# A packed block's second half one fill later, and the kept rows stored one a turn

## The chip, the cores and the metric

The kernel runs on one core of a Trainium2 chip. The metric is the device time of one execution in microseconds. The core has a matrix engine (PE), a vector engine (DVE), an activation engine (ACT), a GpSimd engine and a synchronising engine (SP). In this kernel SP issues all loads and ACT all stores; sixteen DMA engines move the data of both.

## The reference

`x` is one picture of 384 x 384 positions with 384 channels, in bf16 (113 MB). Every channel is averaged and maximised over all positions, a small two-layer network turns the two vectors into one scale per channel, and the picture is multiplied by it.

```python
def reference(x, w1, w2):
    B, H, W, C = x.shape
    xf = x.reshape(B, H * W, C)
    gap = jnp.mean(xf, 1)
    gmp = jnp.amax(xf, 1)
    h_a = gap @ w1
    h_a = h_a * (h_a > 0)
    ...
    scale = _sigmoid(h_a @ w2 + h_m @ w2)
    return x * scale[:, None, None, :]
```

## The kernel before

The 147,456 positions are laid over 128 partitions, 1152 "rows" in each. One row is 768 bytes in each partition, 98,304 bytes in all. The scale is known only when all rows have been seen, and not all rows fit on the chip, so there are two passes: pass one loads everything and keeps as much as it can; pass two multiplies and stores what was kept, and loads the rest again.

**Pass one.** The tile `body` has 96 rows of ring (three slots of 31 rows and a few spare) and seven homes of 24 rows. A list `steps` is written in order by hand; SP issues its loads, PE adds up each loaded piece (`sums`, L258), DVE takes its maximum into `acc` (L324). A slot is loaded again when PE's sums and DVE's maxima over its last contents are done. Loads into the ring are called fills.

Besides the ring there are seven packed blocks (`PACKED`) of 32 rows: 24 go into `homes[i]`, eight into `fourth[i]`, a part of the tile `held`. ACT tests each block (`test`, L285 and L286, three calls) whether its bytes may be packed. PE and ACT then pack it in two halves: `pack(i, half)` is 24 matmuls into the PSUM tile `words_ps` (L306), two ACT copies (L312) and one ACT instruction that reads `words_ps` out (L313). There is one `words_ps`, so PE can begin the second half only behind L313 of the first. After packing, 32 rows lie in 24. All engines run in program order, so where `pack(i, 1)` stands in `steps` sets what PE does before it. Between the blocks stand the fills of `BETWEEN`: the last block (i = 6) is followed by fills of 30 and 27 rows; then come those of `PASSING` (25 rows; 22; 21 and 10 in one slot; 8 and 17 in one slot). From there on slots are loaded for good, piece by piece (`STAYING`, `LAST_HELD`).

Some rows are also kept in PSUM: `kept_ps` (8 rows), `kept_b` (2 rows) and `late` (8 rows, transposed).

**Between the passes** the maximum is folded, the network is evaluated and `scale_bc` is made (L416).

**Pass two.** First the rows that stayed are multiplied and stored. Then 25 turns follow. Turn t multiplies the next reloaded block (L421), stores it (L473), issues every further load whose place is free (`read`, L508), and does that turn's jobs: unpacking a half of a packed block (`unpack`, L451 to L470), or `finish`, which multiplies an unpacked block (24 rows in its home, eight in `held`) and stores it. The sizes and places in `body` of the reloaded blocks are in `PLACES`; the last turns have 48 (turn 18), 48, 48, 48, 36, 30 and 20 rows (turn 24). Block 5 is finished in turn 18, block 6 unpacked in turns 17 and 19 and finished in turn 21. The rows from PSUM are brought back in turn 22: multiplied into rows 222 to 240 of `body`, which lie in the home of block 5. Their three stores and the two of block 6 are issued in the last turn (24), ahead of that turn's own store.

Every DMA signals on one of eight semaphores. The program gives them out in turn, so that a DMA also waits until the one that last had its semaphore has landed.

Of the kernel before, what the change touches and what calls it, by code (L numbers as in the profile page):

```python
# [17 lines left out]
U32 = mybir.dt.uint32  # L18
# [16 lines left out]
PACKED = 7  # L35
PSUM_ROWS = 8
# [22 lines left out]
)  # L59
LEAVING_AT = 222  # L60
FIRST_STORES = ((1, 2, 3, 4, 4, 5, 6, 6), (9, 10, 12), (16, 18))
HELD_STORES = (6, 7)
ACC_STORES_AT = 3
# [6 lines left out]
def kernel(  # L70
# [7 lines left out]
    nc = tc.nc  # L78
# [14 lines left out]
    def rows_of(ap, block):  # L93
        first, n = block
        return ap[first * P:(first + n) * P, :].rearrange("(p n) c -> p n c", n=n)
# [8 lines left out]
    def take(n):  # L104
        nonlocal at
        at += n
        return at - n, n

    ps_block = take(PSUM_ROWS)
    beside = take(BANK_ROWS + A)  # L110
    packed_block = take(GP * PACKED)
    held_block = take(sum(LAST_HELD))
# [7 lines left out]
    again = [take(n) for _, n in PLACES]  # L120
# [25 lines left out]
    body = xpool.tile([P, RING + 3 * G * PACKED, C], BF16, name="body")  # L146
# [13 lines left out]
    kept_ps = psum.tile([P, PSUM_ROWS, C], BF16)  # L160
    words_ps = psum.tile([P, G, C], BF16)
    words = words_ps.rearrange("p n c -> p (n c)").bitcast(F32)
    late = words_ps[:, 0:LATE_ROWS, :]
# [7 lines left out]
    kept_b = bank_b[:, 0:C * BANK_ROWS // 2].bitcast(BF16).rearrange("p (n c) -> p n c", n=BANK_ROWS)  # L171
# [31 lines left out]
    def fill(*parts):  # L203
        nonlocal n_slot
        j = 0
        for block, lo, hi in parts:
            steps.append(("load", block, slots[n_slot % NS][:, j:j + hi - lo, :], lo, hi))
            j += hi - lo
            assert j <= SLOT
        n_slot += 1  # L210

    def whole(block):
        return block, 0, block[1]

    for i in range(PACKED):
        first, d_at = 3 * G * i, 3 * G * PACKED + G * i
        for lo, hi in ((0, FIRST_LOAD), (FIRST_LOAD, 3 * G)) if i == 0 else ((0, 3 * G),):
            steps.append(("load", packed_block, homes[i][:, lo:hi, :], first + lo, first + hi))
        steps.append(("load", packed_block, fourth[i], d_at, d_at + G))
        steps += [("test", i, 0), ("pack", i, 0), ("test", i, 1), ("test", i, 2)]  # L220
        for k, b in enumerate(between[i]):
            if i == 0 and k == 0:
                fill(whole(ps_block), whole(beside), whole(b))
            else:
                fill(whole(b))
            if k == 0:
                steps.append(("pack", i, 1))
    for k, b in enumerate(passing[:-1]):
        if k == SHARED_FILL:
# [96 lines left out]
    def turn_over(out_, rows):  # L326

        for r in range(LATE_ROWS):
            for q in range(CQ):
                nc.tensor.transpose(  # L330
                    out=out_[:, r, q * P:(q + 1) * P], in_=rows[:, r, q * P:(q + 1) * P], identity=ident_bf
                )
# [11 lines left out]
    for st in steps:  # L344
# [8 lines left out]
        _, block, rows, lo, hi = st  # L353
# [9 lines left out]
        j = max(0, min(m, A - done))  # L363
# [41 lines left out]
    for q0, part_ps in tp_ps:  # L405
        n = part_ps.shape[1]
# [12 lines left out]
    def multiply(dst, src):  # L419
        n = dst.shape[1]  # L420
        nc.vector.tensor_tensor(  # L421
            out=dst, in0=src, in1=scale_bc.unsqueeze(1).to_broadcast([P, n, C]), op=ALU.mult
        )

    def put(block, buf, pieces, lo=0):
        j = 0
        for m in pieces:
            rows = buf[:, j:j + m, :]
            multiply(rows, rows)
            nc.scalar.dma_start(out=rows_of(orr, block)[:, lo + j:lo + j + m, :], in_=rows)  # L430
            j += m

    def put_acc():
        for lo, hi in acc_pieces:
            multiply(acc[:, lo:hi, :], acc[:, lo:hi, :])
            nc.scalar.dma_start(out=acc_rows(orr, lo, hi), in_=acc[:, lo:hi, :])


    turns = len(PLACES)
# [32 lines left out]
    def store(buf, block, lo):  # L472
        nc.scalar.dma_start(out=rows_of(orr, block)[:, lo:lo + buf.shape[1], :], in_=buf)  # L473
# [3 lines left out]
    def finish(i):  # L477

        for rows in (homes[i], homes_d[i]):
            multiply(rows, rows)  # L480
        if i < PACKED - 1:
            store_block(i)

    def store_block(i):
        store(homes[i], packed_block, 3 * G * i)
        store(homes_d[i], packed_block, d_at + G * i)


    jobs = [[(unpack, 0, 0)], [(unpack, 0, 1)]]
    for i in range(1, PACKED):  # L490
        jobs += [[(unpack, i, 0)], [(finish, i - 1)], [(unpack, i, 1)]]
    jobs += [[], [(finish, PACKED - 1)]]

    order = []
    turn_of_row = [-1] * (RING + 3 * G * PACKED)

    def read(last_turn, blocks_gone):

        if not again:
            return False  # L500
        k = len(PLACES) - len(again)
        lo, n = PLACES[k]
        if lo + n > RING + 3 * G * blocks_gone or max(turn_of_row[lo:lo + n]) > last_turn:
            return False
        turn_of_row[lo:lo + n] = [k] * n
        buf, b = body[:, lo:lo + n, :], again.pop(0)
        assert b[1] == n
        nc.sync.dma_start(out=buf, in_=rows_of(xr, b))  # L508
        order.append((b, buf))
        return True  # L510

    k = ACC_STORES_AT
    put(stay[0], slots[0], FIRST_STORES[0][:k])
    put_acc()
    j = sum(FIRST_STORES[0][:k])
    put(stay[0], slots[0][:, j:, :], FIRST_STORES[0][k:], j)
    put(held_block, held[:, LATE_ROWS:, :], HELD_STORES, LATE_ROWS)
    put(refill, held[:, 0:LATE_ROWS, :], (LATE_ROWS,))
    read(-1, 0)
    put(stay[1], slots[1], FIRST_STORES[1])  # L520
    read(-1, 0)
    put(stay[2], slots[2], FIRST_STORES[2])
    read(-1, 0)
# [4 lines left out]
    leaving = []  # L528
    gone = 0
    for turn in range(turns):  # L530
        b, buf = order.pop(0)
        multiply(buf, buf)
        if turn == turns - 1:
            for to, block, rows in leaving:
                store(to, block, 0)
            store_block(PACKED - 1)
        store(buf, b, 0)
        while read(turn, gone):
            pass
        for job, *which in jobs.pop(0) if jobs else ():  # L540
            job(*which)
            gone += job is finish
        if turn == turns - 3:
            j = LEAVING_AT
            assert j >= max(lo + n for lo, n in PLACES) and gone > PACKED - 2
            for block, rows in ((held_block, late), (ps_block, kept_ps[:, 0:PSUM_ROWS, :]), (beside, kept_b)):
                n = rows.shape[1]
                to = body[:, j:j + n, :]
                if block == held_block:
                    nc.vector.tensor_copy(out=to.bitcast(U32), in_=rows.bitcast(U32))  # L550
                    turn_over(rows, to)
                leaving.append((to, block, rows))
                j += n
            assert j <= RING + 3 * G * (PACKED - 1)
            for to, block, rows in leaving[1:] + leaving[:1]:
                multiply(to, rows)
    assert not again and not order
    with tc.If(bad != 0):
        for i in range(PACKED):
            for buf, lo in ((homes[i], 3 * G * i), (homes_d[i], d_at + G * i)):  # L560
                n = buf.shape[1]
# [33 lines left out]
```

## Time and profile before

| | us |
|---|---|
| median of 3 runs (734.73 to 735.58) | 735.13 |
| the profiled execution, its own time | 735.08 |
| its span, first to last instruction | 733.3 |
| DVE busy | 563.3 |
| ACT busy | 348.7 |
| PE busy (matmuls) | 187.4 |

The profile's lines are read so: each instruction carries the line of the program that made it, the tile it writes and reads, and its shape; "[2.99 <-DMA ...]" is the time for which its engine stood idle before it, and what ended that. A load or store is seen at its issue, and its landing is told from the issue on. The span begins with the first instruction; 1.8 us of the profiled execution's time lie around it.

### The profile page before, as it was taken

The numbers are of one execution on the slowest core, as the hardware profiler recorded it, in microseconds if no ns is written. First come the engines' busy times: TensorE is split into PE (matmuls) and PEld (weight loads), VectorE is DVE, ScalarE is ACT, GpSimd is POOL, SyncE is SP. The second block draws the span as 40 slices with busy tenths as digits, with TensorE's granted clock in tenths as the row PEclk, the third lists the DMA queues.
The fourth block names the chain that finished last, engine by engine and source line by source line (L and its number), as shares of the span: only waits on it lengthen the run. The fifth ranks groups of instructions, "written<-read, shape, count | busy, mean of one in ns | idle before, by whom it ended". The sixth has DMA issues, their size and how long they took to land.

```text
span 733.3 us, 3860 instructions
## 1 busy us (share of the span) xinstructions
PE 187.4 (26%) x1357; PEld 74.5 (10%) x1357; DVE 563.3 (77%) x421; ACT 348.7 (48%) x251; POOL 0.7 (0%) x6
## 2 busy tenths in 40 slices
PE   5655578676667561000000000000000000001000
PEld 2222223232222130000000000000000000001000
DVE  6799999999998998959999594985866790599110
ACT  6979999999999000046245335081080062000000
POOL 0000000000000000000000000000000000000000
PEclk9989878798977555555555555555555555555555
DMA  9999999999998988999999999999999999999996
GB/s 379 435 422 425 433 430 428 431 428 427 424 430 336 424 345 333 387 431 434 433 430 434 424 438 433 427 436 426 435 431 439 423 444 427 421 434 433 424 422 276
DMA packets 21987, 305.63 MB, mean 417 GB/s; under 512 B 2800, under 2 KB 3408, under 8 KB 9552
## 3 DMA queue, kind: packets, MB, share of 16 engines
q1 hardware_dynamic: 13328, 192.14, 62.0%
q10 hardware_dynamic: 8640, 113.25, 36.3%
q8 instruction: 10, 0.16, 0.1%
q14 instruction: 9, 0.07, 0.0%
HBM read 192.14 MB, written 113.25 MB: 416 GB/s over the span
## 4 chain that ended last, share of the span: by engine, by line
DMA 54%; DVE 18%; another core or an unknown queue 9%; ACT 7%; PE 5%; issue 2%; SPq 0%; ACTq 0%; DVEq 0%
DMA body<-in_x_dram 32%; DMA out_dram<-body 22%; DVE acc L324 8%; DVE body L421 8%; PE words_ps L306 4%; ACT body L312 2%; ACT held L285 2%; ACT held L286 1%; PE bank_a L258 1%; ACT body L313 1%; DVE held L421 0%; ACT body L470 0%; ACT held L470 0%; DVE acc L421 0%
## 5 line engine op out<-in xcount | busy, mean ns | idle before, releaser
L421 DVE TENSOR_TENSOR body<-body,scale_bc 128x9216 bf16<-128x9216 bf16 (+15 forms) x45 | 214.7, 4803 | 106.4 <-DMA body<-in_x_dram 103.6
L324 DVE TENSOR_TENSOR acc<-acc,body 128x2304 bf16<-128x2304 bf16 (+4 forms) x210 | 229.8, 1166 | 17.3 <-DMA body<-in_x_dram 17.3
L470 ACT COPY held<-body 128x1536 uint8<-128x1536 uint8 x14 | 20.6, 1475 | 201.4 <-DMA out_dram<-held 130.6
L258 PE MATMUL bank_a<-body,small 128*1 128x512 bf16 (+2 forms) x849 | 85.6, 453 | 67.4 <-DMA body<-in_x_dram 67.4
L330 PE MATMUL words_ps<-ident_bf,body 128*128 128x128 bf16 x24 | 2.7, 309 | 387.6 <-DVE body L550 387.6
L286 ACT ACTIVATE held<-held 128x3072 uint8<-128x3072 uint8 (+1 forms) x35 | 82.0, 2343 | 1.1
L285 ACT ACTIVATE held<-body,held 128x3072 uint8<-128x3072 int8 (+1 forms) x28 | 61.9, 2211 | 10.3 <-DMA body<-in_x_dram 9.8
L306 PE MATMUL words_ps<-body,scale_bc 128*128 128x512 fp8e4 (+1 forms) x126 | 40.4, 436 | 24.4 <-ACT body L313 24.4
L258 PEld LDWEIGHTS <-small 128*1 128x1 bf16 x891 | 29.5, 93 | 125.9 <-issue 107.0
L330 PEld LDWEIGHTS <-body 128*128 128x128 bf16 x24 | 2.5, 143 | 387.9 <-issue 387.9
L470 ACT COPY body<-acc 128x1536 uint8<-128x1536 uint8 x28 | 41.2, 1472 | 0.4
L306 PE MATMUL words_ps<-body,w_sb 128*128 128x512 fp8e3 x84 | 28.1, 419 | 0.0
L306 PE MATMUL words_ps<-held,body 128*128 128x512 fp8e4 x84 | 27.3, 409 | 0.0
L470 ACT COPY held<-acc 128x1536 uint8<-128x1536 uint8 x14 | 20.6, 1472 | 7.2 <-DVE acc L456 7.2
L470 ACT COPY body<-body 128x1536 uint8<-128x1536 uint8 x14 | 20.7, 1475 | 0.4
L312 ACT COPY body<-held 128x1536 uint8<-128x1536 uint8 x14 | 20.6, 1469 | 0.0
L470 ACT COPY acc<-body 128x1536 uint8<-128x1536 uint8 x14 | 20.5, 1466 | 0.0
L312 ACT COPY body<-body 128x1536 uint8<-128x1536 uint8 x14 | 20.4, 1460 | 0.0
L313 ACT ACTIVATE body<-words_ps 128x1536 uint16<-128x1536 f32 x14 | 20.1, 1439 | 0.0
L285 ACT ACTIVATE held<-held 128x3072 uint8<-128x3072 int8 x7 | 20.0, 2855 | 0.2
L306 PEld LDWEIGHTS <-scale_bc 128*128 128x128 bf16 x126 | 13.1, 107 | 46.9 <-issue 36.9
L324 DVE TENSOR_TENSOR acc<-acc,held 128x1920 bf16<-128x1920 bf16 (+4 forms) x18 | 17.5, 1008 | 0.1
(70 smaller groups left out, 183.2 us busy)
## 6 DMA issues: line engine op xcount, KB each, us to landing
body<-in_x_dram SPq DMA_DIRECT2D x20, 2976.0 KB, 21.7
out_dram<-body ACTq DMA_DIRECT2D x17, 2304.0 KB, 29.6
body<-in_x_dram SPq DMA_DIRECT2D x16, 2304.0 KB, 17.9
body<-in_x_dram SPq DMA_DIRECT2D x4, 4608.0 KB, 27.8
out_dram<-body ACTq DMA_DIRECT2D x4, 4608.0 KB, 47.3
body<-in_x_dram SPq DMA_DIRECT2D x6, 2880.0 KB, 20.1
body<-in_x_dram SPq DMA_DIRECT2D x5, 3456.0 KB, 20.2
out_dram<-body ACTq DMA_DIRECT2D x5, 3456.0 KB, 43.1
```

The source lines that it names most:

```text
L258: nc.tensor.matmul(sum_ps[q * QP:q * QP + 1, 0:g * P], lhsT=ones_bf[:, 0:1], rhs=rows[:, k:k + g, q * P:(q + 1) * P], start=(done + k == 0 ...
L285: nc.scalar.activation(out=out_, in_=rows, func=ACT.Square, bias=test_bias, scale=TEST_SCALE)
L286: nc.scalar.activation(out=out_, in_=out_, func=ACT.Square, bias=minus4, accum_out=tests[:, k:k + 1],)
L306: nc.tensor.matmul(words[:, c:c + BANK], lhsT=weights[2 * r + k], rhs=high(part(i, r), dt)[:, half * n + c:half * n + c + BANK], start=(r ...
L312: nc.scalar.copy(out=high(part(i, r), U8)[:, span], in_=low(part(i, r + 2), U8)[:, span])
L313: nc.scalar.activation(out=part(i, 2).rearrange("p n c -> p (n c)").bitcast(U16)[:, span], in_=words, func=ACT.Copy, bias=32767.5,)
L324: nc.vector.tensor_tensor(out=out_, in0=in0, in1=in1, op=ALU.max)
L330: nc.tensor.transpose(out=out_[:, r, q * P:(q + 1) * P], in_=rows[:, r, q * P:(q + 1) * P], identity=ident_bf)
L421: nc.vector.tensor_tensor(out=dst, in0=src, in1=scale_bc.unsqueeze(1).to_broadcast([P, n, C]), op=ALU.mult)
L470: nc.scalar.copy(out=dst, in_=src)
```

## The change

In pass one the second half of a block's packing is put behind the second fill after the block, where it stood behind the first. In pass two the rows from PSUM are multiplied three turns earlier (turn 19), in another order of places; their stores are issued one a turn in turns 20, 21 and 22, each behind that turn's own store; and block 6 is stored where it is finished, in turn 21. The last turn stores its own block alone.

```diff
+LEAVING_TURN = 19
...
-            if k == 0:
+            if k == 1:
                 steps.append(("pack", i, 1))
...
         for rows in (homes[i], homes_d[i]):
             multiply(rows, rows)
-        if i < PACKED - 1:
-            store_block(i)
-
-    def store_block(i):
         store(homes[i], packed_block, 3 * G * i)
         store(homes_d[i], packed_block, d_at + G * i)
...
         multiply(buf, buf)
-        if turn == turns - 1:
-            for to, block, rows in leaving:
-                store(to, block, 0)
-            store_block(PACKED - 1)
         store(buf, b, 0)
+        if leaving:
+            to, block = leaving.pop(0)
+            store(to, block, 0)
         while read(turn, gone):
             pass
...
-        if turn == turns - 3:
+        if turn == LEAVING_TURN:
             j = LEAVING_AT
-            for block, rows in ((held_block, late), (ps_block, kept_ps[:, 0:PSUM_ROWS, :]), (beside, kept_b)):
+            for block, rows in ((ps_block, kept_ps[:, 0:PSUM_ROWS, :]), (held_block, late), (beside, kept_b)):
                 n = rows.shape[1]
-                to = body[:, j:j + n, :]
-                if block == held_block:
-                    nc.vector.tensor_copy(out=to.bitcast(U32), in_=rows.bitcast(U32))
-                    turn_over(rows, to)
-                leaving.append((to, block, rows))
+                leaving.append((body[:, j:j + n, :], block))
                 j += n
-            for to, block, rows in leaving[1:] + leaving[:1]:
-                multiply(to, rows)
+            to = leaving[1][0]
+            nc.vector.tensor_copy(out=to.bitcast(U32), in_=late.bitcast(U32))
+            turn_over(late, to)
+            multiply(leaving[0][0], kept_ps[:, 0:PSUM_ROWS, :])
+            multiply(leaving[2][0], kept_b)
+            multiply(to, late)
```

The same instructions are issued before and after; only their order changes. Behind turn 19's unpacking DVE now has the copy out of `late` (L550 in the profile before) and the three multiplications of the PSUM rows, ahead of the multiplication of turn 20.

More of the change, by code (lines that the diff above doesn't have):

```diff
@@ L491 @@
         jobs += [[(unpack, i, 0)], [(finish, i - 1)], [(unpack, i, 1)]]
-    jobs += [[], [(finish, PACKED - 1)]]
+    jobs.append([])
+    jobs.append([(finish, PACKED - 1)])
     order = []
@@ L542 @@
             gone += job is finish
-        if turn == turns - 3:
+        if turn == LEAVING_TURN:
             j = LEAVING_AT
             assert j >= max(lo + n for lo, n in PLACES) and gone > PACKED - 2
-            for block, rows in ((held_block, late), (ps_block, kept_ps[:, 0:PSUM_ROWS, :]), (beside, kept_b)):
+            for block, rows in ((ps_block, kept_ps[:, 0:PSUM_ROWS, :]), (held_block, late), (beside, kept_b)):
                 n = rows.shape[1]
-                to = body[:, j:j + n, :]
-                if block == held_block:
-                    nc.vector.tensor_copy(out=to.bitcast(U32), in_=rows.bitcast(U32))
-                    turn_over(rows, to)
-                leaving.append((to, block, rows))
+                leaving.append((body[:, j:j + n, :], block))
                 j += n
             assert j <= RING + 3 * G * (PACKED - 1)
-            for to, block, rows in leaving[1:] + leaving[:1]:
-                multiply(to, rows)
-    assert not again and not order
+            to = leaving[1][0]
[4 more added lines that the diff above has]
+            multiply(to, late)
+    assert not again and not order and not jobs and not leaving
     with tc.If(bad != 0):
```

## The prediction

> **What bounds the kernel now.** I read the page's slices first, then the windows around the one dip they show, then the chain there, and last the engines' timelines at the dip and at the end.
>
> ```profile
> span 733.3 us, 3860 instructions
> DMA  9999999999998988999999999999999999999996
> GB/s 379 435 422 425 433 430 428 431 428 427 424 430 336 424 345 333 387 431 434 433 430 434 424 438 433 427 436 426 435 431 439 423 444 427 421 434 433 424 422 276
> ...
> 110.00:226.00 116.00, 85.50 (x546) 31.62 (x546) 110.05 (x103) 115.06 (x77) 0.00 (x0) 0.81 1.00 428
> 226.00:230.00 4.00, 4.00 (x44) 1.64 (x45) 4.00 (x5) 3.94 (x4) 0.00 (x0) 1.00 0.30 125
> ...
> 650.00:673.00 23.00, 2.72 (x24) 2.48 (x24) 22.23 (x9) 0.00 (x0) 0.00 (x0) 0.50 1.03 441
> 673.00:695.00 22.00, 0.00 (x0) 0.00 (x0) 5.61 (x2) 0.00 (x0) 0.00 (x0) 0.50 1.00 423
> 720.00:733.30 13.30, 0.00 (x0) 0.00 (x0) 0.00 (x0) 0.00 (x0) 0.00 (x0) 0.50 0.51 218
> ```
>
> The last two columns of a window are the DMA share and GB/s. The kernel is bound by its DMA engines: full nearly throughout at 420 to 440 GB/s. An edit can gain only where they stand idle. They do so in the 13th slice (220 to 238 us, 336 GB/s), between the passes (15th to 17th), and in the last one. At 428 GB/s a row of 98,304 bytes takes 0.23 us; that is my price for a row.
>
> The first dip is sharp: from 226 to 230 us the engines are busy 30% of the time. The chain of waits tells why.
>
> ```profile
> 206.69 7.58 PE words_ps L306 x24
> ...
> 219.80 7.83 PE words_ps L306 x24
> 227.64 2.93 PE bank_a L258 x42
> ...
> 230.58 15.47 DMA body<-in_x_dram
> ```
>
> This is block 6: the first half's matmuls at 206.7, the second half's from 219.8 to 227.6, and behind them the sums of 42 matmuls that had queued up. They are those of the fills of 27 and 25 rows, and a slot is not loaded again before its sums are made.
>
> ```profile
> L355 SPq DMA_DIRECT2D body<-in_x_dram x1: 328/328/328, 196.5 to 196.5; - x1
> DMA to landing us min/median/max: 21.5/21.5/21.5
> ...
> L355 SPq DMA_DIRECT2D body<-in_x_dram x1: 328/328/328, 216.8 to 216.8; - x1
> DMA to landing us min/median/max: 12.0/12.0/12.0
> ...
> L355 SPq DMA_DIRECT2D body<-in_x_dram x1: 328/328/328, 229.1 to 229.1; - x1
> DMA to landing us min/median/max: 8.0/8.0/8.0
> ...
> 221.95 2.22 DVE L324 TENSOR_TENSOR acc<-acc,body 128x1920 bf16<-128x1920 bf16 x2
> ...
> 237.18 8.44 DVE L324 TENSOR_TENSOR acc<-acc,body 128x2304 bf16<-128x2304 bf16 x8 [2.99 <-DMA body<-in_x_dram]
> 246.15 2.43 DVE L324 TENSOR_TENSOR acc<-acc,body 128x2304 bf16<-128x2304 bf16 x2 [0.53 <-DMA body<-in_x_dram]
> ```
>
> The 27 rows landed at 218.0 (196.5 + 21.5), DVE was done with them at 224.2 (the row at 221.95 ends there), but PE's sums ended only at about 229. So the next load, 21 rows into that slot, went out at 229.1, after the load before it (22 rows) had landed at 228.8 and the queue was empty. It landed at 237.1: 8.3 us after its predecessor where its rows cost 4.8. DVE, which had kept up with every landing, stood idle for 2.99 us, and for 0.53 us again when the 17 rows of the next slot came in. Apart from these it runs back to back until the maximum is complete. That maximum releases the scale and with it all of pass two.
>
> **The packing edit.** PE's order for block 6 becomes: first half, sums of 30 rows, sums of 27 rows, second half, sums of 25 rows. The 27 rows land at 218.0. Their sums are 21 matmuls, at 2.93/42 = 0.07 us each 1.5 us, so done at 219.6. The slot is then released by DVE at 224.2, and the load of 21 rows goes out 4.9 us earlier, while 22 rows are still coming in until 228.8. The second half still begins at 219.8, where the first half's L313 lets it, and ends at 227.6; the sums of 25 rows come next and end at about 229.2, not later than before. DVE's maxima over these rows, at 6.71 us for 31 rows (row below), end at 224.2 + 5.4 = 229.6, and the following slot (8 and 17 rows) goes out then. By then 31 rows, 7.1 us of DMA work, are queued. The queue no longer runs dry: the 21 rows land at 228.8 + 4.8 = 233.6, before DVE is free at 237.18 - 2.99 = 234.2; the 17 rows land 56 rows behind 228.8, at 241.7, before DVE would want them at 246.15 - 0.53 - 2.99 = 242.6. Both idle times go: **3.5 us**, all on the path, since DVE sets the end of pass one and pass two hangs on it. What is late next is DVE itself.
>
> A load into an empty queue costs more than its rows, 8.0 us against 4.8 here, and that surplus is the larger part of the dip. The Trainium skill (DMA: Bandwidth & Descriptors, Anatomy of one DMA) gives for transfers on GpSimd's path about 2.0 us fixed and the bytes at 436 GB/s. By it the 21 rows would take an estimated 6.7 us; the trace's 8.0 decides, but by the page's figure the gain would be 2.2 us and the time 732.9.
>
> For blocks 0 to 5 I cost the edit at nothing, for the engines are full from 110 to 226 us (share 1.00). What the cover must bear:
>
> ```profile
> 119.13 6.71 DVE acc L324 x6
> ...
> 218.31 1.44 ACT L313 ACTIVATE body<-words_ps 128x1536 uint16<-128x1536 f32 x1
> 234.56 1.46 ACT L312 COPY body<-body 128x1536 uint8<-128x1536 uint8 x1
> ...
> 227.57 4.16 PE L258 MATMUL bank_a<-body,small 128*1 128x512 bf16 x60
> ```
>
> Up to 7.8 us of matmuls now stand between the sums of the second fill and those of the third. A fill of 31 rows lands 7.1 us behind the one before and DVE then needs 6.7 us for it, so the third slot is not released by DVE until 13.8 us behind the second landing; PE needs about 1.8 + 7.8 + 1.8 = 11.4. ACT wants the second half's matmuls 16.2 us after it began the first half's L313 (218.31 to 234.56), as it has three tests between; block 6 has them at 227.6. If that cover failed, ACT, busy 115 of 116 us, would slip by the same amount.
>
> **The stores.** Nothing changes until turn 19's unpacking ends. Then:
>
> ```profile
> 604.41 0.96 DVE L456 SCALAR_TENSOR_TENSOR body<-body,held 128x768 uint32<-128x768 uint32 x1
> 623.13 9.76 DVE L421 TENSOR_TENSOR body<-body,scale_bc 128x18432 bf16<-128x18432 bf16 x1 [17.77 <-DMA body<-in_x_dram]
> 642.38 14.63 DVE L421 TENSOR_TENSOR body<-body,scale_bc 128x18432 bf16<-128x18432 bf16 x2 [9.50 <-DMA body<-in_x_dram]
> 656.93 1.75 DVE L421 TENSOR_TENSOR held<-held,scale_bc 128x3072 bf16<-128x3072 bf16 x1
> 658.60 7.35 DVE L421 TENSOR_TENSOR body<-body,scale_bc 128x13824 bf16<-128x13824 bf16 x1
> 665.87 1.75 DVE L550 COPY body<-words_ps 128x1536 uint32<-128x1536 uint32 x1
> 670.52 1.76 DVE L421 TENSOR_TENSOR body<-words_ps,scale_bc 128x3072 bf16<-128x3072 bf16 x1 [0.77 <-PE words_ps L330]
> 672.19 6.15 DVE L421 TENSOR_TENSOR body<-body,scale_bc 128x11520 bf16<-128x11520 bf16 x1
> 694.73 4.16 DVE L421 TENSOR_TENSOR body<-body,scale_bc 128x7680 bf16<-128x7680 bf16 x1 [16.39 <-DMA body<-in_x_dram]
> ...
> L473 ACTq DMA_DIRECT2D out_dram<-body x1: 1040/1040/1040, 597.1 to 597.1; - x1
> DMA to landing us min/median/max: 52.0/52.0/52.0
> ...
> L473 ACTq DMA_DIRECT2D out_dram<-body x1: 758/758/758, 600.1 to 600.1; - x1
> DMA to landing us min/median/max: 72.7/72.7/72.7
> ...
> L508 SPq DMA_DIRECT2D body<-in_x_dram x1: 327/327/327, 649.2 to 649.2; - x1
> ...
> 700.94 0.34 ACTq L473 DMA_DIRECT2D out_dram<-body  x1
> ```
>
> The edit adds a wait. The moved copy writes rows 222 to 240, in the home of block 5, whose store went out at 597.1 and lands at 649.1. In turn 22 that was long past; in turn 19 DVE arrives at 605.4 and stands until 649.1, with the multiplications of turns 20 to 24 queued behind it. (Times here are those of the trace of before; the 3.5 us move all alike.) Then: PSUM rows, 665.87 to 672.28, 6.4 us, to 655.5; turn 20 (48 rows, 9.76) to 665.3, 32 us later than before; turn 21 to 675.0, block 6 (4.9 + 1.75) to 681.6; turn 22 to 689.0; turn 23 to 695.1; turn 24, whose load lands at 694.7 as before (DVE starts on it at 694.73), to 699.2.
>
> Does DMA notice? Stores run one behind another. Turn 19's went out at 600.1 and is down at 672.8, so turn 20's, ready at 665.3, still comes 7.5 us early. From 672.8 on the queue is filled as follows, at 0.23 us a row: 48 + 8 rows and the last load's 20 until 690.3, with turn 21's store there since 675.0; that, the transposed rows and block 6 (88 rows in all) until 710.5, with turn 22's there since 689.0; 36 rows until 718.8, with the 2 rows and turn 23's there since 695.1; 32 rows until 726.2, with the last there since 699.2; its 20 rows until about 731, where they end now. The 2-row store has the semaphore of the last load and waits for 694.7 with turn 23's and 24's behind it on ACT; turn 23's multiplication ends no sooner. No load waits for a moved store: the last two wait for block 5's and turn 19's. So the wait costs **0**, between -1 (the last store goes out at 699.2 and not at 700.9) and +1.5 (some of the sixteen engines are through with turn 19's store before turn 20's is there).
>
> **Sum.** 735.08 - 3.5 + 0 = 731.6; the profiled time equals the median within 0.05, so nothing is added. Its own range is 730.6 to 733.6: from 3.5 us and the -1, to 3.0 us (the 0.53 stays) and the +1.5. A measurement of this kernel can tell about 0.2%, 1.5 us, from no change.
>
> **Rivals.** *The dip only moves (about 735.0).* The slot of 8 and 17 rows still waits for sums behind the second half. The queue is covered by 31 rows, to 235.9; a lone load exceeds its rows by 3.2 us (8.0 - 4.8), so from 232.7 on, 3 us behind DVE's release at 229.6, each us of PE's lateness opens the gap again, and at near 7 us nothing is left. For it: PE has only 0.4 us to spare against DVE. Against it: the second half starts when it started, and with PE warm. Chance 0.09.
>
> *DVE held too long (743, slower).* The 7.5 us of lead is all that keeps the stores fed. If the copy's wait is met only by turn 19's store, at 672.8 and not 649.1, turn 20's store goes out at 689.0, 16.2 us after the queue's last store; the last load covers 4.6 of that: 731.6 + 11.6 = 743. It loses from 7.5 us of lateness on, and eats the gain at 11. For it: 44 us of DVE idling are new. Against it: the next load into that home went out at 649.2 (the SP row), so its release is there. Chance 0.11.
>
> *The drain shortens too (728).* In the last 13.3 us the engines are busy 51%. If an earlier last store evens them out by half of those 6.5 us idle, 3 us more are gained. Against it: the store queue never ran dry, so which engine is last was settled long before. Chance 0.06.
>
> **Numbers.** Forecast 0.74. The range, 729.9 to 734.3, takes it in, with a part of the first rival above it and of the third below. Faster: 0.74 + 0.06 = 0.80; same 0.09; slower 0.11.
>
> **What would show it.** Right: no DVE idle of 2.99 us near 234; the load of 21 rows out near 224.3 and the dip at 226 to 230 gone; the scale 3.5 us earlier; an idle time of about 44 us ahead of the copy, and the DMA share from 650 to 695 still 1.0. Wrong: a dip some us later in pass one, or DMA below 0.95 between 660 and 695.

## The result, and the profile after

The changed kernel takes 731.59 us (median of 5 runs, 731.16 to 732.10) against 735.58 for the kernel before in the same session: ratio 0.9947, interval 0.9932 to 0.9961. The forecast was 731.6. The profiled execution took 731.59 us, its span 729.8; that is 3.5 us less than the span before. Line numbers in the new traces are one or two higher or lower than before: `sums` is L259, the maxima L325, the packing's matmuls L307, the multiplication L422, the stores L474.

The page's slices and the windows, as they stood in the prediction for before:

```profile
span 729.8 us, 3860 instructions
DMA  9999999999999979999999999999999999999996
GB/s 381 434 425 419 438 420 439 423 434 425 426 430 423 418 298 356 395 434 425 433 427 438 434 424 429 431 438 425 435 435 428 431 431 443 419 436 425 430 423 293
...
226.00:230.00 4.00, 4.00 (x46) 1.64 (x45) 4.00 (x5) 3.94 (x4) 0.00 (x0) 1.00 0.99 419
650.00:673.00 23.00, 1.11 (x11) 0.85 (x8) 22.23 (x5) 0.00 (x0) 0.00 (x0) 0.50 1.00 432
673.00:695.00 22.00, 0.00 (x0) 0.00 (x0) 22.00 (x5) 0.00 (x0) 0.00 (x0) 0.50 0.99 418
720.00:729.80 9.80, 0.00 (x0) 0.00 (x0) 0.00 (x0) 0.00 (x0) 0.00 (x0) 0.50 0.40 171
```

The dip of pass one is gone: the 13th slice has 423 GB/s where it had 336, and from 226 to 230 us the DMA share is 0.99 where it was 0.30. From 650 to 695 us the engines are as full as before.

The chain of waits around the place where the dip was, the load of 21 rows (its issue and its landing), and DVE's timeline in pass one:

```profile
218.09 3.05 PE bank_a L259 x21
221.14 6.36 PE words_ps L307 x24
227.50 2.12 PE bank_a L259 x28
229.62 13.75 DMA body<-in_x_dram
...
277.62 0.50 ACT scale_bc L417
...
L356 SPq DMA_DIRECT2D body<-in_x_dram x1: 328/328/328, 223.6 to 223.6; - x1
DMA to landing us min/median/max: 10.1/10.1/10.1
...
213.24 29.34 DVE L325 TENSOR_TENSOR acc<-acc,body 128x1920 bf16<-128x1920 bf16 x27
243.47 24.36 DVE L325 TENSOR_TENSOR acc<-acc,body 128x2304 bf16<-128x2304 bf16 x22 [0.89 <-DMA body<-in_x_dram]
```

The sums of the 27 rows now come ahead of the second half's matmuls. The load of 21 rows goes out at 223.6, where it went at 229.1, and lands at 233.7. DVE runs without a break from 213.2 to 242.6: the idle time of 2.99 us is gone. One of 0.89 us is there, where 0.53 was. The chain still passes through the second half's matmuls, but to the next load, that of 17 rows: it goes out at 229.6, when PE's sums of the 25 rows end (229.62) and DVE has just finished with them too (229.55). The scale (the row at 277.62) began at 280.29 before: 2.67 us earlier.

DVE's timeline in pass two:

```profile
646.49 1.76 DVE L549 COPY body<-words_ps 128x1536 uint32<-128x1536 uint32 x1 [43.54 <-DMA out_dram<-body]
...
651.15 1.76 DVE L422 TENSOR_TENSOR body<-words_ps,scale_bc 128x3072 bf16<-128x3072 bf16 x1 [0.77 <-PE words_ps L331]
652.83 24.29 DVE L422 TENSOR_TENSOR body<-body,scale_bc 128x18432 bf16<-128x18432 bf16 x3
677.03 1.75 DVE L422 TENSOR_TENSOR held<-held,scale_bc 128x3072 bf16<-128x3072 bf16 x1
678.70 17.49 DVE L422 TENSOR_TENSOR body<-body,scale_bc 128x13824 bf16<-128x13824 bf16 x3
...
662.61 1.30 ACTq L474 DMA_DIRECT2D out_dram<-body  x2
...
L506 SPq DMA_DIRECT2D body<-in_x_dram x1: 328/328/328, 670.2 to 670.2; - x1
DMA to landing us min/median/max: 17.0/17.0/17.0
```

The copy waits for 43.54 us for the store of block 5, DVE then works without a break to 696.2, turn 20's store goes out at 662.6, and the DMA share stays at 0.99 to 1.00 from 650 to 695 us. The last load lands 17.0 us after its issue where it took 21.8.

### The profile page after: what moved, and what is told of

Read it like the earlier page. It is cut to its first block, busy times and chain, and to the rows that moved or that the text cites. A ratio compares the mean times of both kernels' runs of the same rounds, so it can differ in the third digit from the quotient of the medians.

```text
span 729.8 us, 3860 instructions
## 1 busy us (share of the span) xinstructions
PE 186.4 (26%) x1357; PEld 73.0 (10%) x1357; DVE 563.1 (77%) x421; ACT 348.7 (48%) x251; POOL 0.7 (0%) x6
## 4 chain that ended last, share of the span: by engine, by line
DMA 59%; DVE 23%; another core or an unknown queue 6%; issue 3%; PE 2%; ACT 1%; SPq 0%; ACTq 0%; DVEq 0%
DMA body<-in_x_dram 42%; DMA out_dram<-body 17%; DVE body L422 11%; DVE acc L325 10%; PE words_ps L307 1%; PE bank_a L259 1%; DVE held L422 1%; ACT body L471 0%; ACT held L471 0%; SPq L356 0%; PE words_ps L331 0%; DVE acc L422 0%; DVE held L452 0%; DVE body L549 0%
## 5 line engine op out<-in xcount | busy, mean ns | idle before, releaser
L422 DVE TENSOR_TENSOR body<-body,scale_bc 128x9216 bf16<-128x9216 bf16 (+15 forms) x45 | 214.5, 4802 | 63.0 <-DMA body<-in_x_dram 60.2
L325 DVE TENSOR_TENSOR acc<-acc,body 128x2304 bf16<-128x2304 bf16 (+4 forms) x210 | 229.7, 1166 | 14.6 <-DMA body<-in_x_dram 14.5
L259 PE MATMUL bank_a<-body,small 128*1 128x512 bf16 (+2 forms) x849 | 93.0, 481 | 83.8 <-DMA body<-in_x_dram 83.7
L259 PEld LDWEIGHTS <-small 128*1 128x1 bf16 x891 | 30.4, 96 | 147.1 <-issue 131.6
L307 PE MATMUL words_ps<-body,scale_bc 128*128 128x512 fp8e4 (+1 forms) x126 | 37.4, 409 | 3.7 <-ACT body L314 3.7
L549 DVE COPY body<-words_ps 128x1536 uint32<-128x1536 uint32 x1 | 1.8, 1757 | 43.5 <-DMA out_dram<-body 43.5
L307 PE MATMUL words_ps<-body,w_sb 128*128 128x512 fp8e3 x84 | 26.0, 392 | 0.0
L307 PE MATMUL words_ps<-held,body 128*128 128x512 fp8e4 x84 | 25.0, 379 | 0.0
L314 ACT ACTIVATE body<-words_ps 128x1536 uint16<-128x1536 f32 x14 | 20.1, 1438 | 0.0
L325 DVE TENSOR_TENSOR acc<-acc,held 128x1920 bf16<-128x1920 bf16 (+4 forms) x18 | 17.5, 1008 | 0.1
## 6 DMA issues: line engine op xcount, KB each, us to landing
body<-in_x_dram SPq DMA_DIRECT2D x6, 2880.0 KB, 20.1
```

Source lines behind the costliest of these rows:

```text
L259: nc.tensor.matmul(sum_ps[q * QP:q * QP + 1, 0:g * P], lhsT=ones_bf[:, 0:1], rhs=rows[:, k:k + g, q * P:(q + 1) * P], start=(done + k == 0 ...
L307: nc.tensor.matmul(words[:, c:c + BANK], lhsT=weights[2 * r + k], rhs=high(part(i, r), dt)[:, half * n + c:half * n + c + BANK], start=(r ...
L314: nc.scalar.activation(out=part(i, 2).rearrange("p n c -> p (n c)").bitcast(U16)[:, span], in_=words, func=ACT.Copy, bias=32767.5,)
L325: nc.vector.tensor_tensor(out=out_, in0=in0, in1=in1, op=ALU.max)
L422: nc.vector.tensor_tensor(out=dst, in0=src, in1=scale_bc.unsqueeze(1).to_broadcast([P, n, C]), op=ALU.mult)
L549: nc.vector.tensor_copy(out=to.bitcast(U32), in_=late.bitcast(U32))
```

## The experiments

My theory after this: the gain is pass one's, through the last block alone; the wait of 44 us on DVE is free. The rivals: the stores carry a part of it, or the wait costs something that the earlier stores hide; and for the 0.89 us that stayed, the dip has moved behind the 31 rows.

### The parts alone

Packing alone (first run): only this edit in the kernel before.

```diff
-            if k == 0:
+            if k == 1:
                 steps.append(("pack", i, 1))
```

> The packing edit alone, the stores as before. Theory (the gain is pass one's): the load of 21 rows goes out near 223.6 us, the scale is ready about 2.7 us earlier (280.3 to 277.6) and the time falls by 2.7 us, ratio 0.9963. If pass two's order carried a share of its own, the end moves no more than the scale does. Rival (the stores carry the gain): within 1 us of before.

The stores alone: the changed kernel with `k == 0` put back.

> The stores' edit alone, the packing as before. Theory: pass one is as before (scale at 280.3), DVE idles about 44 us ahead of the copy, and the time is the same within 1 us; 0.9 us less if the drain at the end is really shorter for it. Rival (the wait costs): 1 to 8 us slower, with the DMA share below 0.95 between 660 and 690 us.

The last block alone, with the stores as before:

```diff
-            if k == 0:
+            if k == (1 if i == PACKED - 1 else 0):
                 steps.append(("pack", i, 1))
```

> The packing edit for the last block alone, stores as before. Theory: all of the gain comes from the last block, so the time equals that of the packing edit for all blocks within 0.5 us, 2.7 us below before. Rival (several blocks bring a share each): about 0.4 us gained, a seventh.

Later all three kernels were taken once more on one chip, as the share of the stores stood open:

> The packing edit alone once more, beside the changed kernel and the stores' edit alone on one chip. Open is whether the stores' edit has a share of its own. If it has none: ratio 0.9950 to 0.9960, the same as the changed kernel within its interval, and the stores' edit alone at 1.000. If it brings 1 us: this at 0.9960, the changed kernel at 0.9947, the stores' edit alone at 0.9985.

> The stores' edit alone once more. No share: within 0.7 us of before. A share of 1 us: 0.9985. In the trace the scale should be ready between 279.3 and 280.3 us and the last stores land where they do in before.

> The changed kernel beside the two parts: 0.9947 again, 3.5 to 4 us below before. The stores' edit has a share if this lies more than 0.7 us below the packing edit alone.

| kernel | ratio to before | interval | median us |
|---|---|---|---|
| packing alone | 0.9969 | 0.9954 to 0.9983 | 732.83 |
| packing alone, again | 0.9964 | 0.9950 to 0.9978 | 732.38 |
| packing of the last block alone | 0.9956 | 0.9940 to 0.9972 | 732.13 |
| stores alone | 0.9983 | 0.9968 to 0.9998 | 734.20 |
| stores alone, again | 0.9978 | 0.9966 to 0.9991 | 733.69 |
| changed kernel, third time | 0.9950 | 0.9934 to 0.9967 | 731.77 |

The packing edit is worth 2.3 and 2.6 us by the ratios, for the last block alone 3.2. That one is 0.7 us faster than all blocks together, where I expected at most 0.5 between them, but the intervals overlap: the last block carries the gain, and the other six bring nothing that can be told. The traces agree. The scale starts at 280.29, 279.31 and 279.54 in the three with the old order (mean 279.71) and between 277.19 and 277.62 in the eleven that pack the last block's second half later (mean 277.41): 2.3 us.

The stores alone are not the same as before: 1.2 and 1.6 us faster, with intervals that leave 1 out both times. The two parts, multiplied, come near the whole (0.9964 x 0.9978 = 0.9942; the whole 0.9947 and 0.9950). That speaks against my first theory, no share for the stores. But the direct comparison doesn't settle it: on one chip the changed kernel lies 0.61 us below the packing alone (731.77 and 732.38), short of the 0.7 I had asked for, and the intervals overlap. So a share of the stores is likely and not shown. The traces don't show one. From the start of the scale to the end of the span it takes 453.0 us in before; 452.8, 452.6 and 451.4 in the three profiled executions with the old stores and the new packing; 452.2, 452.5 and 453.0 in the changed kernel, 454.1 and 453.0 with the new stores alone. These overlap. The cause of the 1.2 to 1.6 us stays open.

What the traces of the stores alone do show is that pass one of the kernel before isn't alike in all executions. Its program up to the scale is that of before, but the scale starts at 279.31 and 279.54, not at 280.29. The windows of the last block's second half, of before and then of the stores alone (the third number from the end is the granted clock):

```profile
222.00:228.00 6.00, 6.00 (x27) 2.19 (x28) 6.00 (x7) 5.90 (x5) 0.00 (x0) 0.76 0.86 365
```

```profile
222.00:228.00 6.00, 6.00 (x41) 2.45 (x42) 6.00 (x7) 5.90 (x5) 0.00 (x0) 0.93 0.86 365
...
L356 SPq DMA_DIRECT2D body<-in_x_dram x1: 328/328/328, 228.1 to 228.1; - x1
...
235.91 8.44 DVE L325 TENSOR_TENSOR acc<-acc,body 128x2304 bf16<-128x2304 bf16 x8 [1.58 <-DMA body<-in_x_dram]
```

PE was granted 0.93 of its clock there and not 0.76, did 41 matmuls in the six microseconds and not 27, and the load went out 1.0 us earlier; DVE's idle time is 1.58 us and not 2.99. The Trainium skill (TensorE: Matmul & The Clock Gate, Part 1: The HAM clock gate) says that PE has half its clock until it has been busy for a window of about 3.4 us, and that the window runs freely, so that the switch falls differently from run to run. These two traces agree: PE begins the second half at 219.8 us in both, and in 1 us windows the granted clock goes from about 0.5 to 1.0 at 224.9 us in before and at 222.8 in the other. With the old order this chance sits on the path that releases the load of 21 rows; with the new one DVE releases it, and the start of the scale varies by 0.43 us over eleven traces, where it varied by 0.98 over three.

### Does the wait cost anything?

Bringing the rows back in turn 20, behind that turn's multiplication:

```diff
-LEAVING_TURN = 19
+LEAVING_TURN = 20
```

> The changed kernel with the PSUM rows brought back in turn 20, behind that turn's multiplication, so that DVE waits less and the multiplication of turn 20 does not stand behind the wait. Theory (the wait of 44 us on DVE is free): the same time as the changed kernel within 0.7 us, 3.5 to 4 us below before. Rival (the wait costs something that the earlier stores hide): 1 to 2 us faster than the changed kernel.

DVE waits 15.1 us in place of 43.5 (row below), the time is 732.69 us, ratio 0.9973 (0.9956 to 0.9989).

```profile
645.52 1.76 DVE L549 COPY body<-words_ps 128x1536 uint32<-128x1536 uint32 x1 [15.11 <-DMA out_dram<-body]
```

It is not faster than the changed kernel (731.30 to 731.77, in other sessions), so the rival falls. My theory isn't met either: it should have lain 3.5 to 4 us below before, and lies 2.0 below by the ratio. By its median it stands beside the packing alone, but its interval also overlaps the changed kernel's. So this run doesn't say whether the time of the stores matters.

How much later may turn 20's store come? Idle maxima on DVE, between the PSUM rows and turn 20, n = 3 and n = 10, beside the changed kernel itself:

```diff
             multiply(to, late)
+            for _ in range(n):
+                maximum(acc, acc, acc)
```

> The changed kernel itself beside two with more work on DVE. Expected 3 to 4 us below before, as first measured (ratio 0.9947). If the stores' edit has a share of its own of about 1 us, the scale is ready 2.7 us earlier and the end comes 3.5 us earlier again; if that was the chance of one execution, the two differ by less or in the other direction.

> The changed kernel with three idle maxima of 11 rows on DVE (2.4 us each, 7.2 us) between the PSUM rows and turn 20's multiplication. Theory (the store queue has a lead of 7.5 us): turn 20's store goes out near 670, when the store of turn 19 lands, and the end moves by 0 to 1 us. Rival (there is no lead, since the faster DMA engines run dry first): 4 to 7 us slower than the changed kernel.

> The same with ten idle maxima, 24 us. Theory: turn 20's store goes out near 686.5, 16.5 us after turn 19's landed; the last load of 20 rows covers 4.6 us of it, so the end comes about 12 us later than in the changed kernel, near 743, and the DMA share from 670 to 690 falls to about 0.3. Rival (the order of the stores has slack of its own, as the multiplications run ahead of the queue): under 5 us.

The changed kernel again has 731.30 us (0.9947, 0.9924 to 0.9969). With three maxima it is 733.32 us (0.9974, 0.9959 to 0.9988), 2.0 us more; with ten 744.62 us (1.0123, 1.0097 to 1.0149), 13.3 us more. The windows of the changed kernel (its execution of the result), of three and of ten maxima:

```profile
660.00:672.00 12.00, 0.00 (x0) 0.00 (x0) 12.00 (x2) 0.00 (x0) 0.00 (x0) 0.50 1.01 436
672.00:690.00 18.00, 0.00 (x0) 0.00 (x0) 18.00 (x5) 0.00 (x0) 0.00 (x0) 0.50 1.03 434
```

```profile
670.25 14.92 ACTq L474 DMA_DIRECT2D out_dram<-body  x5
...
660.00:672.00 12.00, 0.00 (x0) 0.00 (x0) 12.00 (x3) 0.00 (x0) 0.00 (x0) 0.50 0.64 272
672.00:690.00 18.00, 0.00 (x0) 0.00 (x0) 18.00 (x4) 0.00 (x0) 0.00 (x0) 0.50 1.02 413
720.00:732.00 12.00, 0.00 (x0) 0.00 (x0) 0.00 (x0) 0.00 (x0) 0.00 (x0) 0.50 0.76 327
```

```profile
686.78 14.92 ACTq L474 DMA_DIRECT2D out_dram<-body  x5
...
660.00:672.00 12.00, 0.00 (x0) 0.00 (x0) 11.83 (x6) 0.00 (x0) 0.00 (x0) 0.50 0.57 229
672.00:690.00 18.00, 0.00 (x0) 0.00 (x0) 17.93 (x5) 0.00 (x0) 0.00 (x0) 0.50 0.41 167
720.00:742.80 22.80, 0.00 (x0) 0.00 (x0) 0.36 (x1) 0.00 (x0) 0.00 (x0) 0.50 0.92 392
```

The result lies between my two expectations, and the rows say why. With 7.1 us more, turn 20's store goes out at 670.3, as foreseen about when turn 19's lands. But most of the sixteen engines are through with their share of turn 19's earlier (in the trace its sixteen completions lie between 663.7 and 670.7 us), and stand idle: 36% of 12 us, 4.3 us of each. Only 2 us of it reach the end, for the drain becomes shorter in turn: 24% of 12 us idle where the changed kernel has 60% of 9.8 (2.9 us against 5.9). The engines that ran ahead lose their lead first. With 24 us there is no lead left to give, and 13.3 us come through; I had worked out 12, and a DMA share of about 0.3 where the row from 672 to 690 has 0.41. So the rival "DVE held too long" has a true price. It begins below 7 us of lateness: in the changed kernel the first completion of turn 19's store is at 665.0, only 2.4 us after turn 20's store goes out (662.61).

### What the 0.89 us are

Packing the last block's second half behind the third fill (25 rows):

```diff
-            if k == 1:
+            if k == 1 and i < PACKED - 1:
                 steps.append(("pack", i, 1))
     for k, b in enumerate(passing[:-1]):
+        if k == 1:
+            steps.append(("pack", PACKED - 1, 1))
```

> The changed kernel with the last block's second half packed behind the third fill (25 rows), so that the sums of that fill do not stand behind it either. First rival of the prediction (the dip moved behind the 31 rows, as the sums of 25 rows end late at 229.6): the next slot goes out earlier and DVE's idle time of 0.89 us near 243 goes, 0.9 us gained over the changed kernel. Theory: the slot is freed by DVE at 229.5 in any case, the queue is full there, and the idle time has another cause (one of the sixteen DMA engines is late, as PE's instructions are fetched through it near 237): the idle time stays within 0.3 us and the time within 0.5 us.

The time is 731.15 us (0.9941, 0.9920 to 0.9962) beside 731.30 for the changed kernel on the same chip, and DVE still idles:

```profile
243.27 19.21 DVE L327 TENSOR_TENSOR acc<-acc,body 128x2304 bf16<-128x2304 bf16 x17 [0.80 <-DMA body<-in_x_dram]
```

So the idle time isn't made by the sums of the 25 rows; the prediction's first rival falls. The trace of the changed kernel says more: of the sixteen completions of the load of 17 rows fifteen are there by 241.74 and the last at 243.37. In all ten traces that pack the last block's second half later and leave PE's program as it is, the fifteenth comes between 241.68 and 241.94 and the last between 243.04 and 243.37. The trace holds a candidate too: at 237.5 us one packet of 16 KB (1.10 us) goes through the DMA queue that the page calls "instruction". The DMA view of the changed kernel from 236.5 to 239 us has this row:

```profile
q8 instruction: 1, 0.02, 2.8%
```

If it makes one of the sixteen engines late, DVE waits for that one: its maxima begin at 243.47, behind the last completion. PE works through the longest program (1357 matmuls and as many weight loads; DVE has 421 instructions), so I moved its instructions against the loads:

```diff
+    for _ in range(100):
+        nc.tensor.matmul(sum_ps[0:1, 0:P], lhsT=ones_bf[:, 0:1], rhs=ident_bf, start=True, stop=True)
     done = turn = nth = 0
```

> The changed kernel with 100 idle matmuls (200 PE instructions) ahead of the first sums; their result is overwritten. They shift the points at which PE's instructions are fetched through the DMA engines: by the count of instructions the fetch near 237.5 us comes near 219 and that of 269 near 250. Theory (the fetch makes one of the sixteen DMA engines late, and DVE waits for that engine): DVE's idle time of 0.75 to 0.89 us near 243 falls below 0.3, and 0.5 us or more appear behind the new fetch, near 225 or 255; the end within 1 us. Rival (the idle time belongs to the loads of 8 and 17 rows themselves): it stays near 243 at 0.6 to 0.9.

Its DMA view from 217 to 222 us, the load of 25 rows, and DVE's timeline:

```profile
q8 instruction: 1, 0.02, 1.4%
...
L358 SPq DMA_DIRECT2D body<-in_x_dram x1: 328/328/328, 203.7 to 203.7; - x1
DMA to landing us min/median/max: 21.4/21.4/21.4
...
213.22 10.97 DVE L325 TENSOR_TENSOR acc<-acc,body 128x1920 bf16<-128x1920 bf16 x10
225.15 37.42 DVE L325 TENSOR_TENSOR acc<-acc,body 128x1920 bf16<-128x1920 bf16 x34 [0.96 <-DMA body<-in_x_dram]
```

The packet has moved to 221.6 and DVE's idle time with it, to 225.15, with 0.96 us; near 243 there is none. The load of 25 rows takes 21.4 us to land where the changed kernel's takes 20.1. Of its sixteen completions in the trace fifteen are there by 223.76 and the last at 225.06. So the idle time is that of the fetch, as far as one execution can show it. One completion is just as late 18 us on: of the load of 17 rows fifteen completions are there by 241.81 and the last at 243.11. DVE is 0.96 us later itself by then and no longer waits for it. The one run took 731.82 us, and the scale started at 277.51, where it was 277.62: moving the fetch gained nothing.

## Why the prediction was right

**The dip and its release: right.** The load of 21 rows was to go out near 224.3 and went at 223.6, as it needs only the first 21 of the 27 rows in its slot and their maxima end at 223.1; it was to land at 233.6 and landed at 233.7; the idle time of 2.99 us is gone, and the chain there no longer passes through the second half's matmuls to that load. The packing alone, and the last block alone, show the cause by themselves. The 0.4 us that PE had to spare against DVE at the next slot were used up (229.62 against 229.55), and with the queue full that cost nothing to be seen.

**The sum of pass one: a term mis-sized.** "Both idle times go: **3.5 us**" was 2.67 in the trace of the changed kernel. The step that failed is "the 17 rows land 56 rows behind 228.8, at 241.7": fifteen engines were through by then (241.74), but the load had landed only at 243.4 (229.62 + 13.75), as one engine was late behind the fetch. The 8 rows were late in the same way (fifteen by 237.81, the last at 239.60), but DVE didn't wait for them. I had taken the stream's rate for the landing, without anything that delays a single engine.

And 3.5 us was read from one trace of before, the one of three with the largest dip: the two others with the old order idle 2.50 and 2.91 us at the two places, not 3.52. Against their mean the gain in the traces is 2.3 us, and in the times 2.3 and 2.6. The 2.2 us by the Trainium skill's figure came out nearer than my 3.5. That is luck: the figure is about what a load into an empty queue costs, and not about an engine that is late.

**A detail of PE: wrong, without weight.** The sums of 27 rows took 3.05 us and not 1.5: PE came to them from 4.17 us of idling, and was granted 0.50 of its clock from 218.0 to 221.1. So the second half began at 221.1 and not at 219.8. It then took 6.36 us and not 7.83, with 0.83 of the clock granted (0.67 in before), and ended at 227.5 as forecast.

**The stores: the wait right, the sum open.** The wait of 44 us is there (43.54). Turn 20's store was to go out at 661.8 (665.3 less 3.5) and went at 662.61, which is 665.3 less the 2.67 us that the scale came earlier. The share from 650 to 695 stayed at 0.99 to 1.00, and the last load went out as soon as turn 19's store had landed (670.2). The cost of 0 was to lie between -1 and +1.5; the times of the stores alone give -1.2 and -1.6, past the lower end, the direct comparison -0.6, and no run tells why. "Whose load lands at 694.7 as before" was wrong: it landed at 687.2, 4.8 us earlier than the shift explains, as it took 17.0 us and not 21.8.

**The total.** That 731.6 was met to a hundredth is luck. By the parts alone, 0.9 to 1.2 us too much for the packing stand against 1.2 to 1.6 too little for the stores. And the kernel before took 735.58 in the session of the result, not the 735.08 that the sum starts from: the gain was 4.0 us where 3.5 was forecast.

**The rivals.** "The dip only moves" didn't come about: the DMA share is 0.99 there, and the time with the second half behind the third fill is the same. "DVE held too long" has about the price it was given (11.6 worked out for 23.7 us of lateness; 13.3 measured for about 24), but it doesn't begin as sharply as I put it, at 7.5 us: 7.1 us of lateness already cost 2.0. Where it begins wasn't measured. "The drain shortens too" isn't shown: the last 13.3 us of before have 6.5 us of idling, the last 13.3 of the changed kernel (share 0.56) 5.9.

## What to carry to other kernels

In a program where every engine runs in order, look at what stands ahead of the small piece of work that releases a buffer. Here 1.5 to 3 us of sums stood behind 7.8 us of matmuls that nobody was yet waiting for, and a load came to its queue 0.3 us after it had run empty; with the order turned round its release hangs on the engine that sets the pace anyway. Read the size of such a dip from several executions: here one trace showed 3.5 us of idling and the others 2.5 and 2.9. A long new wait on an engine is harmless as long as the queue it feeds is filled past the wait's end; work out that lead for the engines that finish first, not only for the landing, which tells of the last one.

## What the runs showed of the hardware that I had not expected

A 16 KB packet on the instruction queue, 1.10 us long, makes one of the sixteen DMA engines 1.3 to 1.6 us late (a load landed 21.4 us after its issue and not 20.1; of another, fifteen completions were there by 241.74 and the last at 243.37), and DVE, without slack, idled for 0.58 to 0.96 us behind it. The last completion stayed about 1.3 us behind the fifteenth over the next five loads (to 243.11 in the run with the fetch moved). When the store queue runs dry for a while, the engines come out level: after 24 us more on DVE the completions of the last store lie within 0.2 us of each other, after 7 us within 1.0, where they lie 5.1 us apart in the changed kernel and 6.2 in before. The DMA share over the last 13.3 us is 0.83, 0.80, 0.56 and 0.51.
